# A prologue's row-max tiles over four PSUM banks instead of three, and a gelu's cube one step later

## The chip, the cores and the metric

The kernel runs on one core of one Trainium2 chip. The metric is the device time of one execution in microseconds (us). The engines are TensorE (PE in the profile; PEld is its weight load), VectorE (DVE), ScalarE (ACT), GpSimd (POOL) and SyncE (SP), which issues the DMAs. Each works through a queue of its own in order, and they wait for each other through semaphores.

## The reference, cut to what matters

```python
x = A_x                                          # (1, 2048, 640)
g = sigmoid((x * gate_w).sum(-1, keepdims=True))
q, k, v = heads(x @ wq), x @ wk, x @ wv          # 32 heads of 20; one k and one v for all heads
p = softmax(q @ k.T * 20 ** -0.5)
a = merge(p @ v) @ wo
h = layernorm(x)                                 # over the 640 channels
u = gelu(einsum("bsd,sf->bdf", h, w1) + b1)      # token mixing: F = 1728
b = transpose(einsum("bdf,fs->bds", u, w2) + b2)
return g * a + (1 - g) * b
```

All of it is float32. Products are made of a high part and a low part of each operand (three products of four).

## The kernel before, in words

**Three stages.** Up to about 96 us in the trace the kernel projects x to q, k, v and normalises it. Then comes a **prologue** (the loop over `fc in range(PRO)`, lines 574 to 601), about 72 us long, and after it the **main loop** (`main`, line 1017, and the blocks behind it), which holds the other 90% of the time. The change touches the prologue alone, and what its tiles leave to the main loop.

**The prologue's PE work.** It makes the first 8 (`PRO`) of 14 blocks of the first half of `u`. One pass of the loop is one block, `fc`: 4 quarters `hf` of 4 steps each, so 16 steps. A step is 6 matmuls (L586) on half the rows of the array each; `pu0` takes the upper rows, `pu1` the lower ones, and at the end of the pass the two are added. One weight chunk serves one quarter. `w1_upto` (line 118) prepares it three quarters ahead: a DMA brings `wr`; ScalarE rounds it to `wh` (L126; from chunk 32 on GpSimd does that, L128); GpSimd makes the rest `wl` = `wr` - `wh` (L129). So in each pass there are four chunks, called A, B, C and D here, prepared at steps 0, 4, 8 and 12.

**The row maxima.** Between steps, `lead` (line 569) starts two matmuls of q against k, 128x512 each (L479), and for each of them VectorE takes the maximum along the row (`tensor_reduce`, L482). There are 48 (`LEAD`) such pairs, so 96 tiles; one pair falls on each second or third step. The tiles come from `next_bank` (line 459), which in the prologue rotates over the pool `ps_m` of three banks. A tile can be written only after the reduction of the tile three earlier.

**PSUM.** The eight banks in the prologue: three for `ps_m`, one for `ps_g`, which stays unused until the main loop, and four for `pu0` and `pu1`, twice each (`psb`). In the main loop the four of `psb` become `ps_s` (three) and `ps_o` (one).

**The gelu.** At the end of each pass `gelu` (line 515) is called. ScalarE first takes `pu0` and the bias (called *bias* below, L519). The rest is put in the list `chain`, of which one entry is taken at the end of each following step (`pop_chain`), so it runs within the next pass. Its entries, with the short names used below:

- *add* (L525, VectorE, adds `pu1`) and right behind it *square* (L522, ScalarE)
- *cube* (L529, VectorE; `scalar_tensor_tensor` with two inputs in SBUF)
- *tanh* (L532, ScalarE)
- *product* (L545 and L546, GpSimd)
- *high* (L535, ScalarE, rounds to `u_hi`)
- *low* (L538, GpSimd)

A `None` is a step in which nothing of the gelu is issued. The last block's gelu (`fc == PRO - 1`) issues its add at once and has another chain, on GpSimd.

**The order of each queue** is thus the order in which the Python code issues (`manual_schedule` on all engines). ScalarE's queue in a pass is: wh of A, square, wh of B, tanh, wh of C, high, wh of D, then *bias* of this pass. GpSimd's is: wl of A, wl of B, product, wl of C, wl of D, low.

**The join.** The first tile from `ps_s` in the main loop (L479, tile `s`) takes a bank of `psb`, and so waits for the add of the last block's gelu, which waits for that block's *bias*, which stands on ScalarE behind *high* of the block before.

Of the kernel before, what the change touches and what calls it, by code (L numbers as in the profile page):

```python
# [9 lines left out]
F32 = mybir.dt.float32  # L10
# [4 lines left out]
PSUM = bass.MemoryType.PSUM  # L15
DRAM = bass.MemoryType.DRAM

P = 128
# [6 lines left out]
NB = 512  # L25
# [14 lines left out]
def mix_kernel(ctx: ExitStack, tc: tile.TileContext, A_x, A_wq, A_wk, A_wv, A_wo,  # L40
# [5 lines left out]
    def f32(ap):  # L46
        return ap.bitcast(F32)
# [30 lines left out]
    right = ExitStack()  # L78
# [39 lines left out]
    def w1_upto(n):  # L118
        while fetched[0] < min(n, len(chunks)):
            c = fetched[0]  # L120
            w1_load(c + 1)
            wr = w1raw[c]
            wh = w1p.tile([P, HS, P], F32R, name="wh")
            wl = w1p.tile([P, HS, P], F32R, name="wl")
            if c < 4 * PRO:
                nc.scalar.activation(wh, wr, AF.Copy)  # L126
            else:
                nc.gpsimd.tensor_copy(wh, wr)  # L128
            nc.gpsimd.tensor_sub(wl, wr, f32(wh))  # L129
            w1t[c] = wh, wl  # L130
            fetched[0] += 1
            w1_load(c + 4)
# [22 lines left out]
    def new_q(n):  # L155
        if n < NU:
            qtiles[n] = load_q(n, "qst")
# [289 lines left out]
    u_lo = [view(t, UC * HD2, UC) for t in (u0, slot[0])]  # L447
    pp_pool = ctx.enter_context(tc.tile_pool(name="pp", bufs=11))
    ev = ctx.enter_context(tc.tile_pool(name="ev", bufs=1))
    ps_m = ctx.enter_context(tc.tile_pool(name="ps_m", bufs=3, space=PSUM))  # L450
    ps_g = ctx.enter_context(tc.tile_pool(name="ps_g", bufs=1, space=PSUM))
    mpool = ctx.enter_context(tc.tile_pool(name="mpool", bufs=2))
    mmpool = ctx.enter_context(tc.tile_pool(name="mmpool", bufs=2))

# [3 lines left out]

    def next_bank():
        if not ring:  # L460
            return ps_m.tile([P, NB], F32, name="ms")
        ring[0] ^= 1
        return ps_m.tile([P, NB], F32, name="ms") if ring[0] else ps_s.tile([P, NB], F32, name="s")
    given = [0, 0]
# [2 lines left out]
    def ms_next(b):  # L467
        k = given[b]
        if k >= 32 * NU:
            return None  # L470
        given[b] += 1
        n, r = divmod(k, 32)
        (kq, pr), qt = divmod(r // 4, 2), r % 4

        def step():
            if n not in mtiles:
                mtiles[n] = mpool.tile([P, 16, 4], F32, name="mp")
            ms = next_bank()
            nc.tensor.matmul(ms, qmax[n][64 * b:64 * b + 60, pr, qt * P:(qt + 1) * P],  # L479
                             kst[64 * b:64 * b + 60, kq * NB:(kq + 1) * NB], start=True, stop=True)  # L480
            c = (2 * b + pr) * 4 + qt
            nc.vector.tensor_reduce(mtiles[n][:, c, kq:kq + 1], ms, axis=AX.X, op=ALU.max)  # L482
            issued[b] += 1
            if min(issued) == 32 * n + 1:
                new_qmax(n + 1)

        return step

    def ms_done():
        n = len(row_max)  # L490
        if n < NU and min(issued) >= 32 * (n + 1):
            mm = mmpool.tile([P, 16], F32, name="mm")
            nc.vector.tensor_reduce(mm, mtiles.pop(n), axis=AX.X, op=ALU.max)
            mn = mmpool.tile([P, 2, 16], F32R, name="mn")
            nc.gpsimd.tensor_scalar(mm, mm, -1.0, None, op0=ALU.mult)
            nc.gpsimd.tensor_copy(mn[:, 0, :], mm)
            nc.gpsimd.tensor_sub(mn[:, 1, :], mm, f32(mn[:, 0, :]))
            row_max[n] = mn

    def store_max(n):  # L500
        mn = row_max[n]
        mt = mpool.tile([P, 32], F32, name="mt")
        nc.vector.transpose(mt, f32(mn).rearrange("p j c -> p (j c)"))
        nc.sync.dma_start(out=m_scr[n], in_=mt)

    def fetch_max(n):
        src = m_scr[n].rearrange("(i j b r) e -> j b r i e", j=2, b=2, r=8)
        for b in range(2):
            for j in range(2):
                rows = f32(qtiles[n][64 * b + 60 + j:64 * b + 61 + j])  # L510
                nc.sync.dma_start(out=rows.rearrange("o p (t i e) -> o (p t) i e", i=4, e=32), in_=src[j, b][None])

    chain = []

    def gelu(d, fc, accs):
        both = fin.tile([P, D], F32, name="yo")
        xg, t1 = both[:, :HD2], both[:, HD2:]
        hi, lo = u_hi[d][:, fc, :], u_lo[d][:, fc, :]
        nc.scalar.activation(xg, accs[0][:, :HD2], AF.Identity, bias=bias[:, NS + fc:NS + fc + 1])  # L519

        def square():
            nc.scalar.activation(t1, xg, AF.Square)  # L522

        def add():
            nc.vector.tensor_add(xg, xg, accs[1][:, :HD2])  # L525
            square()

        def cube():
            nc.vector.scalar_tensor_tensor(t1, t1, 1.0 / 0.044715, xg, op0=ALU.add, op1=ALU.mult)  # L529

        def tanh():
            nc.scalar.activation(t1, t1, AF.Tanh, scale=GC * 0.044715)  # L532

        def high():
            nc.scalar.activation(hi, t1, AF.Copy)  # L535

        def low():
            nc.gpsimd.tensor_sub(lo, t1, f32(hi))  # L538

        def cube_p():  # L540
            nc.gpsimd.tensor_scalar(t1, t1, 1.0, 1.0 / 0.044715, op0=ALU.mult, op1=ALU.add)
            nc.gpsimd.tensor_mul(t1, t1, xg)

        def prod_p():
            nc.gpsimd.tensor_scalar(t1, t1, 1.0, 1.0, op0=ALU.mult, op1=ALU.add)  # L545
            nc.gpsimd.tensor_mul(t1, t1, xg)  # L546

        def high_p():
            nc.gpsimd.tensor_copy(hi, t1)
            nc.gpsimd.tensor_sub(lo, t1, f32(hi))  # L550

        if len(accs) == 2 and fc == PRO - 1:
            add()
            chain.extend((cube_p, None, tanh, prod_p, high_p))
        elif len(accs) == 2:
            chain.extend((None, None, add, None, cube, tanh, None, prod_p, None, None, None, high, None, low))
        else:
            chain.extend((square, cube_p, None, tanh, prod_p, high_p))

    def pop_chain():  # L560
        f = chain.pop(0) if chain else None
        if f:
            f()

    with tc.tile_pool(name="psb", bufs=2, space=PSUM, side="right") as psb:
        at, skip, last = 0, 3, NS * PRO - 6
        one_by_one[0] = True

        def lead():
            for b in range(2):  # L570
                ms_next(b)()
            ms_done()

        for fc in range(PRO):
            pu = [psb.tile([P, NB], F32, name=f"pu{r}") for r in range(2)]
            for hf in range(4):
                w1_upto(4 * fc + hf + 4)
                for f in [q_parts_due.pop(0) for _ in range(min(len(q_parts_due), 1 + fc // 5))] if fc else []:
                    f()
                wh, wl = w1t.pop(4 * fc + hf)  # L580
                for c in range(HS):
                    st = hf * HS + c
                    for k, (w, h) in enumerate(((wh, h_hi[0]), (wh, h_lo[0]), (wl, h_hi[0]))):
                        for r in range(2):
                            rows = slice(64 * r, 64 * r + 64)
                            nc.tensor.matmul(pu[r][:, :HD2], w[rows, c, :], h[rows, st, :],  # L586
                                             start=(st == 0 and k == 0), stop=(st == NS - 1 and k == 2))
                    done = [max(0, min(x, last) - skip) * LEAD // (last - skip) for x in (at, at + 1)]
                    if done[1] > done[0]:
                        lead()  # L590
                    at += 1
                    pop_chain()
                if fc == 1 and hf == 0:
                    new_q(0)
                if fc == PRO - 2 and hf == 2:
                    assert not q_parts_due
                    one_by_one[0] = False
                    fetch_max(0)
            gelu(0, fc, pu)
            if fc == PRO - 3:  # L600
                store_max(0)

    ps_s = ctx.enter_context(tc.tile_pool(name="ps_s", bufs=3, space=PSUM))
    ps_o = ctx.enter_context(tc.tile_pool(name="ps_o", bufs=1, space=PSUM))

# [558 lines left out]
```

## Time and profile before

| what | us |
|---|---|
| median of 3 runs | 1671.76 |
| lowest and highest | 1671.31, 1671.92 |
| the profiled execution | 1671.47 |
| its span in the trace | 1669.7 |
| prologue, first matmul of L586 to the start of the last | 96.5 to 168.1 |
| first matmul of tile `s` in the main loop | 169.53 |

All times in the text are counted from the start of the span. The granted TensorE clock is 1.00 throughout. In a row of the timeline the first number is the start and the second the length of one instruction or of a run of equal ones; what stands in square brackets is the idle time of the engine ahead of it and who ended it. Successive instructions of VectorE, ScalarE and GpSimd overlap a little: the next one starts before the row of the last one ends.

### The profile page before, as it was taken

What the parts mean: (1) busy time and instruction counts of PE and PEld (TensorE: products, weight loads), DVE (VectorE), ACT (ScalarE), POOL (GpSimd) and SP (SyncE); (2) the same over time, 40 slices, a digit from 0 to 9 for tenths busy, and PEclk for the clock granted to TensorE, in tenths of its full rate; (3) what the DMA queues carried; (4) which work ended last, traced back from release to release, by engine and by line L of the source; (5) the groups of instructions that cost most, each with busy time, mean ns of one, the idle gap of its engine ahead of it and who ended that gap; (6) DMA issues with size and microseconds to landing.
All of it is one profiled execution on the core that took longest, in us unless ns stands there. A gap on an engine that the chain in (4) does not pass through costs nothing.

```text
span 1669.7 us, 38827 instructions
## 1 busy us (share of the span) xinstructions
PE 1661.0 (99%) x14865; PEld 1105.5 (66%) x14865; DVE 1435.7 (86%) x2732; ACT 1188.0 (71%) x2346; POOL 606.3 (36%) x759
## 2 busy tenths in 40 slices
PE   9999999999999999999999999999999999999998
PEld 7899666666666666666666666666666566666665
DVE  6689899999989999988888988988888998988933
ACT  4434777777777777777777777777777777777775
POOL 6578555455455554422232332122122220111210
PEclk9999999999999999999999999999999999999999
DMA  7665222222132232222222222212222121333611
GB/s 211 205 176 137 79 71 69 78 58 78 53 84 73 71 82 74 58 60 62 66 75 74 55 62 66 61 52 71 63 66 60 55 65 41 96 111 113 189 51 39
DMA packets 178305, 138.20 MB, mean 83 GB/s; under 512 B 33306, under 2 KB 144055, under 8 KB 178119
## 3 DMA queue, kind: packets, MB, share of 16 engines
q1 hardware_dynamic: 177830, 135.39, 28.9%
q8 instruction: 117, 1.92, 0.5%
q14 instruction: 70, 0.57, 0.1%
q10 hardware_dynamic: 288, 0.33, 0.1%
HBM read 102.36 MB, written 31.65 MB: 80 GB/s over the span
## 4 chain that ended last, share of the span: by engine, by line
PE 95%; issue 2%; DVE 1%; SPq 1%; ACT 0%; DMA 0%; POOL 0%; POOLq 0%; DVEq 0%; ACTq 0%
PE o L684 28%; PE ms L479 18%; PE s L657 13%; PE g L750 10%; PE g L929 7%; PE ms L657 5%; PE pp L298 4%; PE s L479 3%; PE pu L586 3%; PE g L875 2%; DVE mp L482 1%; PE ms L831 0%; ACT p L660 0%; PE pt L290 0%; SPq L195 0%
## 5 line engine op out<-in xcount | busy, mean ns | idle before, releaser
L482 DVE TENSOR_REDUCE mp<-ms 128x1 f32<-128x512 f32 x1514 | 967.2, 685 | 130.2 <-PE ms L479 102.7
L660 ACT ACTIVATE p<-s 128x512 f32<-128x512 f32 x1512 | 820.6, 606 | 299.4 <-PE s L657 280.2
L479 PE MATMUL ms<-kst,qmx 60*128 60x512 f32 x1514 | 646.5, 433 | 1.7 <-DVE mp L482 1.7
L657 PE MATMUL s<-qst,kst 62*128 62x512 f32 x1512 | 601.6, 403 | 0.0
L684 PE MATMUL o<-p,v_sb 128*32 128x512 f32 x4096 | 511.3, 601 | 0.0
L479 PEld LDWEIGHTS ms<-kst,qmx 60*128 60x128 f32 x1514 | 279.0, 184 | 244.9 <-ACT p L660 114.7
L482 DVE TENSOR_REDUCE mp<-s 128x1 f32<-128x512 f32 x534 | 355.6, 683 | 12.0 <-PE s L479 11.8
L660 ACT ACTIVATE p<-ms 128x512 f32<-128x512 f32 x536 | 305.1, 599 | 56.8 <-PE ms L657 50.2
L657 PEld LDWEIGHTS s<-qst,kst 62*128 62x128 f32 x1512 | 278.5, 186 | 55.2 <-DVE flag L670 31.0
L929 PE MATMUL g<-slot,wh 64*128 64x320 f32 x1280 | 297.5, 311 | 0.0
L129 POOL TENSOR_TENSOR wl<-wr,wh 128x512 fp32r<-128x512 f32 x176 | 228.6, 1300 | 43.8 <-PE g L750 17.3
L479 PE MATMUL s<-kst,qmx 60*128 60x512 f32 x534 | 230.8, 441 | 0.4 <-DVE yo L525 0.4
L684 PEld LDWEIGHTS o<-p,v_sb 128*32 128x32 f32 x4096 | 97.5, 108 | 185.3 <-issue 177.2
L657 PE MATMUL ms<-qst,kst 62*128 62x512 f32 x536 | 216.8, 405 | 0.0
L929 PEld LDWEIGHTS g<-slot,wh 64*128 64x128 f32 x1280 | 211.6, 184 | 2.0 <-issue 1.7
L750 PE MATMUL g<-slot,wh 64*128 64x320 f32 x864 | 202.1, 313 | 0.1
L750 PE MATMUL g<-u,wh 64*128 64x320 f32 x864 | 201.7, 312 | 0.0
L929 PE MATMUL g<-slot,wl 64*128 64x320 f32 x640 | 199.6, 312 | 0.0
L706 POOL TENSOR_TENSOR ot<-ot,rl 128x512 f32<-128x512 f32 x30 | 31.6, 1052 | 346.6 <-DVE rl L705 346.6
L128 POOL CAST wh<-wr 128x512 fp32r<-128x512 f32 x144 | 88.3, 613 | 188.0 <-PE g L750 81.5
L750 PEld LDWEIGHTS g<-slot,wh 64*128 64x128 f32 x864 | 143.5, 184 | 4.9 <-ACT yo L758 4.0
L750 PEld LDWEIGHTS g<-u,wh 64*128 64x128 f32 x864 | 143.5, 184 | 1.1 <-issue 1.1
(202 smaller groups left out, 2092.8 us busy)
## 6 DMA issues: line engine op xcount, KB each, us to landing
wr<-in_B_w_dram SPq DMA_DIRECT2D x152, 256.0 KB
qmx<-q_scr SPq DMA_DIRECT2D x192, 80.0 KB
qst<-q_scr SPq DMA_DIRECT2D x192, 80.0 KB
slot<-o_scr SPq DMA_DIRECT2D x20, 320.0 KB
y_scr<-yo SPq DMA_DIRECT2D x16, 320.0 KB
o_scr<-oh SPq DMA_DIRECT2D x124, 40.0 KB
o_scr<-ol SPq DMA_DIRECT2D x124, 40.0 KB
q_scr<-qh SPq DMA_DIRECT2D x19, 256.0 KB
```

The source lines that it names most:

```text
L128: nc.gpsimd.tensor_copy(wh, wr)
L129: nc.gpsimd.tensor_sub(wl, wr, f32(wh))
L298: nc.tensor.matmul(pp, w, t, start=first and n == 0, stop=not more and n == len(steps) - 1)
L479: nc.tensor.matmul(ms, qmax[n][64 * b:64 * b + 60, pr, qt * P:(qt + 1) * P], kst[64 * b:64 * b + 60, kq * NB:(kq + 1) * NB], start=True, s ...
L482: nc.vector.tensor_reduce(mtiles[n][:, c, kq:kq + 1], ms, axis=AX.X, op=ALU.max)
L586: nc.tensor.matmul(pu[r][:, :HD2], w[rows, c, :], h[rows, st, :], start=(st == 0 and k == 0), stop=(st == NS - 1 and k == 2))
L657: nc.tensor.matmul(s, kst[64 * b:64 * b + 62, kb * P:(kb + 1) * P], q[64 * b:64 * b + 62, pr, :], start=True, stop=True)
L660: nc.scalar.activation(p, s, AF.Exp, scale=SCALE)
L684: nc.tensor.matmul(o[32 * hh:32 * hh + 32, :], v_sb[:, kb, :], ptiles.pop((u, hh)), start=(kb == 0), stop=(kb == NS - 1), skip_group_check ...
L750: other_tile(half, nc.tensor.matmul(hold["p"][:, :HD2], w[r, fc % HS, :], u[d][r, fc, :], start=(hold["n"] == 1), stop=(hold["n"] == 6 * F ...
L875: other_tile(half, nc.tensor.matmul(hold["p"][:, :HD2], o[r, c, :], w[r, c, d * HD2:(d + 1) * HD2], start=(hold["n"] == 1), stop=(hold["n" ...
L929: other_tile(half, nc.tensor.matmul(hold["p"][:, :HD2], w[r, st % HS, :], h[d][r, st, :], start=(hold["n"] == 1), stop=(hold["n"] == 6 * NS)))
```

## The change

```diff
-    ps_m = ctx.enter_context(tc.tile_pool(name="ps_m", bufs=3, space=PSUM))
-    ps_g = ctx.enter_context(tc.tile_pool(name="ps_g", bufs=1, space=PSUM))
...
     def next_bank():
         if not ring:
-            return ps_m.tile([P, NB], F32, name="ms")
+            return psl.tile([P, NB], F32, name="ml")
...
         elif len(accs) == 2:
-            chain.extend((None, None, add, None, cube, tanh, None, prod_p, None, None, None, high, None, low))
+            chain.extend((None, None, add, None, None, cube, tanh, None, prod_p, None, None, high, None, low))
...
-    with tc.tile_pool(name="psb", bufs=2, space=PSUM, side="right") as psb:
+    with tc.tile_pool(name="psl", bufs=4, space=PSUM) as psl, \
+            tc.tile_pool(name="psb", bufs=2, space=PSUM, side="right") as psb:
...
+    ps_m = ctx.enter_context(tc.tile_pool(name="ps_m", bufs=3, space=PSUM))
+    ps_g = ctx.enter_context(tc.tile_pool(name="ps_g", bufs=1, space=PSUM))
     ps_s = ctx.enter_context(tc.tile_pool(name="ps_s", bufs=3, space=PSUM))
```

The prologue's tiles (now called `ml`) come from a pool of four banks, `psl`, which takes the place of `ps_m` and `ps_g`; these two are opened behind the prologue, on the same banks. In the gelu's chain, cube, tanh and product each stand one step later than before; add, high and low stay at theirs. The lists of instructions on PE, ScalarE and SyncE keep their order. On VectorE the cubes of the second and of the fourth block stand behind four reductions after their add instead of two, that of the seventh behind two instead of none; the other four keep their place. On GpSimd the product of each of the seven blocks stands behind wl of C instead of ahead of it. The main loop's code is unchanged.

## The prediction

> **What bounds the kernel now.** First the windows: they say where TensorE is not full, and so where a change can count.
>
> ```profile
> core 0: us, PE busy (x) PEld busy (x) DVE busy (x) ACT busy (x) POOL busy (x), PEclk, DMA share, GB/s
> 96.00:168.00 72.00, 70.28 (x866) 67.66 (x866) 67.50 (x120) 29.36 (x58) 57.39 (x58) 1.00 0.56 154
> 168.00:180.00 12.00, 11.59 (x105) 8.52 (x105) 8.89 (x17) 9.12 (x19) 9.82 (x12) 1.00 0.60 158
> 180.00:200.00 20.00, 20.00 (x188) 13.14 (x185) 18.02 (x37) 14.96 (x31) 7.23 (x11) 1.00 0.12 35
> 400.00:1500.00 1100.00, 1099.81 (x9982) 705.78 (x9980) 990.84 (x1879) 819.75 (x1611) 346.99 (x441) 1.00 0.24 67
> ```
>
> The main loop (last two rows) has PE busy throughout and GpSimd idle for two thirds, so it passes on one for one what the prologue ends earlier or later, and takes up lateness of GpSimd. In the prologue (first row) PE lacks 1.7 us, but VectorE is busy 67.5 of 72 and GpSimd 57.4. Next the list of waits of 96 to 170 us:
>
> ```profile
> ACT u L535 <- POOL yo L546: 10.8, 7, 1.6
> PEld ms L479 <- DVE mp L482: 3.1, 5, 1.4
> PE ms L479 <- DVE mp L482: 1.7, 4, 1.1
> ```
>
> PE and its weight load wait in the prologue for reductions alone: a third bank isn't free. The first row matters later: *high* waits about 1.5 us for the product in each of 7 passes.
>
> How much could PE gain? Three neighbouring pairs from the chain of waits:
>
> ```profile
> 102.05 0.37 PE ms L479 x2
> ...
> 104.73 0.37 PE ms L479 x2
> ...
> 107.40 0.37 PE ms L479 x2
> ```
>
> ```profile
> 106.21 1.19 PE pu L586 x16
> ...
> L586 PE MATMUL pu<-slot,wh x512: 301/305/418, 96.5 to 167.9; 64*128 64x320 f32 x171
> ```
>
> Two pairs with their 5 steps take 2.68 undisturbed, and 16 matmuls 1.19, so a step of six 0.45. The 48 pairs with 120 steps are 24 x 2.68 = 64.3, the 8 other steps 3.6: 67.9 us. From 96.5 PE would end at 164.4 instead of 168.1: **3.7 us** is all that banks can give.
>
> **The change: the fourth bank.** VectorE's share of a pass:
>
> ```profile
> 102.31 2.48 DVE L482 TENSOR_REDUCE mp<-ms 128x1 f32<-128x512 f32 x4 [0.19 <-PE ms L479]
> 115.60 0.48 DVE L525 TENSOR_TENSOR yo<-yo,pu 128x320 f32<-128x320 f32 x1
> 115.99 1.28 DVE L482 TENSOR_REDUCE mp<-ms 128x1 f32<-128x512 f32 x2
> 117.19 0.48 DVE L529 SCALAR_TENSOR_TENSOR yo<-yo 128x320 f32<-128x320 f32 x1
> ```
>
> Four reductions take 2.48, 0.60 from start to start; add and cube push the next one back by 0.4 each. Per 2.68 of PE VectorE thus needs 2.40, and the 0.8 of the gelu is caught up in three such periods of a pass. With three banks the second tile of a pair waits for the first reduction of the pair just before; with four for that of the second last, one reduction (0.60) more of slack. That covers add or cube alone, and the two together in part. Taken alone the edit is worth nearly the 3.7 us.
>
> **The change: cube, tanh and product one step later.** No instruction is added. A cube that follows two more reductions is late by 1.2 us in the second and fourth block. In the seventh it no longer waits for *square* (0.54 in the row of 162.63 below). All this would be small, but the product now stands behind wl of C on GpSimd, and that closes a ring. The rows of the first gelu, GpSimd and then ScalarE:
>
> ```profile
> 108.96 1.65 POOL L129 TENSOR_TENSOR wl<-wr,wh 128x512 fp32r<-128x512 f32 x1 [1.72 <-ACT wh L126]
> 110.58 0.46 POOL L545 TENSOR_SCALAR yo<-yo 128x320 f32<-128x320 f32 x1
> 111.12 0.88 POOL L546 TENSOR_TENSOR yo<-yo 128x320 f32<-128x320 f32 x1
> 111.96 2.54 POOL L129 TENSOR_TENSOR wl<-wr,wh 128x512 fp32r<-128x512 f32 x2
> 114.46 0.88 POOL L538 TENSOR_TENSOR u<-yo,u 128x320 fp32r<-128x320 f32 x1
> 115.30 1.30 POOL L129 TENSOR_TENSOR wl<-wr,wh 128x512 fp32r<-128x512 f32 x1
> 117.18 1.65 POOL L129 TENSOR_TENSOR wl<-wr,wh 128x512 fp32r<-128x512 f32 x1 [0.58 <-ACT wh L126]
> ```
>
> ```profile
> 112.03 0.47 ACT L535 ACTIVATE u<-yo 128x320 fp32r<-128x320 f32 x1 [1.55 <-POOL yo L546]
> 112.41 0.62 ACT L126 ACTIVATE wh<-wr 128x512 fp32r<-128x512 f32 x1
> ...
> 116.48 0.61 ACT L126 ACTIVATE wh<-wr 128x512 fp32r<-128x512 f32 x1
> ```
>
> From start to start a wl takes 1.25, *low* 0.84; the product takes 1.42 from its start to its end (110.58 to 112.00). *High* begins 0.03 later, wh of D 0.38 after that and lasts 0.62, and wl follows 0.08 behind its wh (116.48 + 0.61 to 117.18). So from the product's end to wl of D it is 1.11. Before, wl of C ran in that time. Now wl of C has gone ahead, and GpSimd stands idle. Its pass becomes 1.11 + 1.25 (D) + 0.84 + 3 x 1.25 (A, B, C) + 1.42 = **8.37**, against PE's (67.9 / 8) 8.5: no slack is left, and one more thing is on the ring, the tanh ahead of wh of C, and so the cube. The cube meets GpSimd:
>
> ```profile
> 66.61 1.15 DVE L242 TENSOR_TENSOR r<-r 128x4 f32<-128x4 f32 x1
> 67.80 0.16 DVE L243 TENSOR_TENSOR r<-r,ve 128x4 f32<-128x4 f32 x1
> 162.63 0.78 DVE L529 SCALAR_TENSOR_TENSOR yo<-yo 128x320 f32<-128x320 f32 x1 [0.54 <-ACT yo L522]
> ```
>
> ```profile
> 66.46 1.29 POOL L129 TENSOR_TENSOR wl<-wr,wh 128x512 fp32r<-128x512 f32 x1 [2.31 <-ACT wh L126]
> 161.76 1.29 POOL L129 TENSOR_TENSOR wl<-wr,wh 128x512 fp32r<-128x512 f32 x1
> ```
>
> An operation worth 0.16 that began 0.15 behind a wl ended with it, and the cube that began inside a wl ended 0.36 behind it (163.41 and 163.05). Where cube and wl begin together (117.19 and 117.18), the wl pays, 1.65 instead of 1.29. Before, that is the usual case. Now GpSimd runs without gaps and the cube falls into the middle of a wl. I take it that it waits to that wl's end. [...]
>
> Now the passes, by the product's end. First: wl of C at 110.58, product at 111.83, end **113.25**.
>
> - *Second (cube behind four reductions).* wl of D 114.36, low 115.61, wl of A 116.45, of B 117.70 to 118.99. Add at 115.5, about as before; cube 0.4 + 4 x 0.60 later, at 118.3, inside that wl, so it ends 119.35. Tanh 119.38, wh of C 119.76 to 120.38, wl of C 120.46, product 121.71 to **123.13**: 9.88.
> - *Third (two reductions).* wl of D 124.24, low 125.49, A 126.33 to 127.62. *Bias* stands behind high and wh of D, so it starts at 123.13 + 0.41 + 0.38 = 123.9, and the add comes at 125.3, as before. Cube 1.6 later at 126.9, inside A, ends 127.98; tanh 128.01; wh of C 128.39 to 129.01; wl of C 129.09, 0.26 later than GpSimd could; product ends **131.76**: 8.63.
> - The fourth is as the second, 9.88; the sixth as the third, 8.63. The fifth has three small GpSimd operations more (L495 to L497, 0.86 together, which swallow the 0.26): 9.23. In the seventh GpSimd also rounds two chunks (L128, 0.68 each, 1.36): 8.37 + 1.36 and some 0.15 of cube: 9.9.
>
> Sum: 113.25 + 2 x 9.88 + 2 x 8.63 + 9.23 + 9.9 = **169.40**, against 165.41 before:
>
> ```profile
> 164.54 0.87 POOL L546 TENSOR_TENSOR yo<-yo 128x320 f32<-128x320 f32 x1
> 168.37 0.53 ACT L519 ACTIVATE yo<-pu,bias 128x320 f32<-128x320 f32 x1 [2.46 <-PE pu L586]
> 168.99 0.49 DVE L525 TENSOR_TENSOR yo<-yo,pu 128x320 f32<-128x320 f32 x1 [2.00 <-ACT yo L519]
> 169.53 0.49 PE L479 MATMUL s<-kst,qmx 60*128 60x512 f32 x1 [0.41 <-DVE yo L525]
> ```
>
> Before, the last *bias* waited for PE. Now it stands behind *high*: 169.40 + 0.03 + 0.38 = 169.81, and tile `s` comes 1.16 behind it as here, at **170.97** instead of 169.53. Behind the waiting `s` all of PE's queue stands still. So PE's gain, wherever it is had, is spent waiting at the join, and **1.4 us** are lost. The profiled execution takes 1671.47 (1.8 of it around the span), so 1672.9; it lies 0.3 under the median of 1671.76 and inside the runs' spread.
>
> Other edits at nothing: `ps_m` and `ps_g` opened later start on banks whose reductions end ahead of 168, under the same wait of PE; the product's lateness touches chunks 33 and 34, whose wl would end near 168 and 171.4 and which the main loop needs behind `s`. If that cover fails, it costs what the chunk is late, at most the few tenths that GpSimd's order leaves.
>
> **The rivals.**
>
> - *The gain stays* (1671.47 - 3.7 = **1667.8**): the ring does not bind and PE ends freely. For it: all PE waits in the list are for banks. [...] Against: wl of C was what filled GpSimd's 1.11, and it is taken out. 0.10.
> - *The cube doesn't wait for wl.* The long passes are then: cube ends 118.78, tanh 118.81, wl of C 119.89, 0.57 sooner, so 9.3; short ones 8.37, with the small operations 8.95, the last 9.73. The product ends at 167.3, `s` comes at 168.8, 0.7 sooner than before: **1670.7**. Against: the two rows. 0.14.
> - *The other side: VectorE loses each encounter.* GpSimd's next instruction is queued already, so the cube could lose a full wl in every pass, from the second on, once GpSimd has no gap. Six passes of 9.88 and 0.58 for the small operations: 113.25 + 59.86 = 173.1, `s` at 174.7, 5.1 later: **1676.6**. Two of the three short passes would do to bring it over 1675.1 (9.88 - 8.63 each). For it: no gap is left before C. Against: at 162.63 it lost 0.30 only, and in short passes tanh hides part. 0.10.
> - That the tiles don't rotate over four would leave the ring's loss and PE's waits together; it would give the forecast's time or some tenths more, and is in its range.
>
> **How the numbers follow.** Forecast 0.66 (1672 to 1674 by itself: add and cube may stand 0.6, one reduction, to either side in each long pass), rivals 0.10, 0.14, 0.10. The range leaves out the first rival and the last, 0.2 together: 1670.4 to 1674.8. A measurement of this kernel tells about 0.2% (3.3 us) from no change: faster is under 1668.4, most of the first rival, 0.08; slower over 1675.1, most of the last, 0.09; the rest, 0.83, is the same.
>
> **What would show it.** In the profile after: product (the line of L546) ending near 113.3, 123.1, 131.8 and 169.4; GpSimd idle about 1.1 ahead of wl of D, ended by wh; VectorE's cubes of 0.8 to 1.1 us instead of 0.48; the last *bias* released by *high* and not by PE; PE idle for about 3 us ahead of the first `s`, and that near 171.0. Wrong would be: `s` ahead of 169, with no such idle time (the ring had slack), or products 8.4 apart (no encounter), or PE waiting for reductions as before (the banks did nothing).

## The result and the profile after

| | before | after |
|---|---|---|
| median of 18 runs each (us) | 1671.58 | 1674.47 |
| lowest to highest | 1671.03 to 1671.92 | 1673.72 to 1675.47 |
| profiled execution; its span | 1671.47; 1669.7 | 1675.47; 1673.7 |

The ratio is 1.0017, 95% interval 1.001 to 1.0024: slower by 2.9 us. The forecast was 1672.9, with a range of 1670.4 to 1674.8. The profiled execution of after is the slowest of its 18, and its prologue begins 0.61 later than before's (97.06 and 96.45, ahead of everything that the change touches), so places in the prologue are compared from the first matmul of L586 (L585 in the changed kernel, whose line numbers stand 1 or 2 off).

The waits of 96 to 172 us of the changed kernel (who waited, for whom; us in total, times, longest):

```profile
ACT u L533 <- POOL yo L544: 23.4, 7, 4.6
...
DVE yo L523 <- ACT yo L517: 3.7, 1, 3.7
...
PE s L477 <- DVE yo L523: 3.2, 1, 3.2
...
PEld ml L477 <- DVE mp L480: 1.2, 3, 0.4
```

PE's waits for the banks of the row maxima are down to 1.2 from 4.8 (its own and its weight load's). *High* now waits 23.4 for the product instead of 10.8, and at the join `s` waits 3.2 for the last add (0.4 before), and that add for the last *bias*. GpSimd in the first three passes that hold a gelu, in the sixth, and at the end:

```profile
109.57 2.89 POOL L129 TENSOR_TENSOR wl<-wr,wh 128x512 fp32r<-128x512 f32 x2 [1.76 <-ACT wh L126]
112.43 0.45 POOL L543 TENSOR_SCALAR yo<-yo 128x320 f32<-128x320 f32 x1
112.97 0.87 POOL L544 TENSOR_TENSOR yo<-yo 128x320 f32<-128x320 f32 x1
114.94 1.29 POOL L129 TENSOR_TENSOR wl<-wr,wh 128x512 fp32r<-128x512 f32 x1 [1.10 <-ACT wh L126]
...
117.03 2.55 POOL L129 TENSOR_TENSOR wl<-wr,wh 128x512 fp32r<-128x512 f32 x2
121.04 1.29 POOL L129 TENSOR_TENSOR wl<-wr,wh 128x512 fp32r<-128x512 f32 x1 [1.46 <-ACT wh L126]
...
122.83 0.87 POOL L544 TENSOR_TENSOR yo<-yo 128x320 f32<-128x320 f32 x1
...
126.90 4.04 POOL L129 TENSOR_TENSOR wl<-wr,wh 128x512 fp32r<-128x512 f32 x3
...
131.44 0.88 POOL L544 TENSOR_TENSOR yo<-yo 128x320 f32<-128x320 f32 x1
...
154.77 4.04 POOL L129 TENSOR_TENSOR wl<-wr,wh 128x512 fp32r<-128x512 f32 x3
...
169.28 0.86 POOL L544 TENSOR_TENSOR yo<-yo 128x320 f32<-128x320 f32 x1
```

The idle time of 1.10 ahead of wl of D is there, ended by wh, and in the second pass 1.46 more ahead of wl of C, which waits for the late cube by way of tanh and wh. In the third and in the sixth pass the wl of A, B and C follow each other without a gap, but take 4.04 (the two of 117.03 take 2.55, and a third from start to start 1.25). VectorE's cubes of the first, second, third and sixth block, and then ScalarE at the end:

```profile
109.58 0.48 DVE L527 SCALAR_TENSOR_TENSOR yo<-yo 128x320 f32<-128x320 f32 x1
...
118.79 1.14 DVE L527 SCALAR_TENSOR_TENSOR yo<-yo 128x320 f32<-128x320 f32 x1
...
127.42 1.11 DVE L527 SCALAR_TENSOR_TENSOR yo<-yo 128x320 f32<-128x320 f32 x1
...
154.65 0.52 DVE L527 SCALAR_TENSOR_TENSOR yo<-yo 128x320 f32<-128x320 f32 x1
```

```profile
170.17 0.47 ACT L533 ACTIVATE u<-yo 128x320 fp32r<-128x320 f32 x1 [4.64 <-POOL yo L544]
170.54 0.51 ACT L517 ACTIVATE yo<-pu,bias 128x320 f32<-128x320 f32 x1
```

The cubes of 1.1 are those that came into a wl; they end 0.35 behind it. The last *bias* has no wait of its own: it stands behind *high*, and *high* behind the product. PE at the join, and then three windows around it (columns: window, length, busy time and instructions of PE, PEld, DVE, ACT, POOL, granted clock, DMA share, GB/s):

```profile
167.47 0.49 PE L477 MATMUL ms<-kst,qmx 60*128 60x512 f32 x1 [0.27 <-DVE mp L480]
...
171.68 0.79 PE L477 MATMUL s<-kst,qmx 60*128 60x512 f32 x1 [3.21 <-DVE yo L523]
```

```profile
165.00:171.50 6.50, 3.20 (x36) 2.68 (x32) 2.77 (x6) 1.36 (x3) 6.18 (x8) 1.00 0.46 124
171.50:174.90 3.40, 3.22 (x18) 3.22 (x19) 2.11 (x4) 1.74 (x4) 3.24 (x5) 0.50 0.47 131
174.90:180.00 5.10, 5.10 (x46) 3.19 (x44) 3.85 (x8) 4.78 (x10) 3.41 (x5) 1.00 0.64 180
```

The middle row was not forecast: behind the idle time the granted clock is 0.50 for 3.41 us, and `s` itself takes 0.79 instead of 0.49.

### The profile page after: what moved, and what is told of

Its sections match the earlier page's. It is cut to its first block, busy times and chain, and to the rows that moved or that the text cites. A ratio compares the mean times of both kernels' runs of the same rounds, so it can differ in the third digit from the quotient of the medians.

```text
span 1673.7 us, 38827 instructions
## 1 busy us (share of the span) xinstructions
PE 1662.6 (99%) x14865; PEld 1107.0 (66%) x14865; DVE 1437.6 (86%) x2732; ACT 1186.9 (71%) x2346; POOL 604.6 (36%) x759
## 4 chain that ended last, share of the span: by engine, by line
PE 92%; DVE 4%; issue 2%; DMA 1%; SPq 0%; ACT 0%; POOL 0%; POOLq 0%; DVEq 0%
PE o L685 28%; PE ms L477 17%; PE s L658 13%; PE g L751 10%; PE g L930 7%; PE ms L658 5%; PE pp L298 4%; DVE mp L480 3%; PE s L477 3%; PE g L876 2%; PE ms L832 0%; PE pp L362 0%; PE pu L585 0%; PE pt L290 0%; DMA xa<-in_A_x_dram 0%
## 5 line engine op out<-in xcount | busy, mean ns | idle before, releaser
L480 DVE TENSOR_REDUCE mp<-ms 128x1 f32<-128x512 f32 x1418 | 908.2, 686 | 127.7 <-PE ms L477 100.5
L477 PE MATMUL ms<-kst,qmx 60*128 60x512 f32 x1418 | 615.7, 435 | 0.3 <-DVE mp L480 0.3
L477 PEld LDWEIGHTS ms<-kst,qmx 60*128 60x128 f32 x1418 | 261.8, 185 | 241.5 <-ACT p L661 114.5
```

## The experiments

**Theory A**: the product behind wl of C closes a ring through *high* and wh of D, which sets the pace and keeps the last *bias*, and so `s`, back. **Rival B**: the late cube that meets a wl is the cause, wherever the product stands. **Rival C**: nothing but the half clock behind the idle time. (These letters have nothing to do with the chunks, which are always called wl of A, wh of D and so on.)

The table counts from the first matmul of the prologue in each profile: the start of the prologue's last matmul, the end of the seventh product, the start of `s`, and of the 101st exponential of the main loop (a fixed place some 70 us behind the join); then PE's idle time ahead of `s`, and how long the clock stood at 0.50 behind it. Times are medians; each ratio is to runs of the kernel before on the same chip. The medians of those runs differ by up to 0.9 (1671.58 for after, 1672.32 for e1 to e4, 1672.48 for e5 to e7, 1671.64 for e8 to e10), so times of different chips are compared by their ratios, and small steps by the places within the profile.

| kernel | PE end | product | `s` | 101st exp | idle | half clock | time | ratio (95%) |
|---|---|---|---|---|---|---|---|---|
| before | 71.63 | 68.95 | 73.08 | 144.74 | 0.41 | 0 | 1671.58 | 1 |
| after | 69.83 | 73.07 | 74.62 | 147.38 | 3.21 | 3.41 | 1674.47 | 1.0017 (1.001 to 1.0024) |
| e1_banks | 69.48 | 67.39 | 70.93 | 142.61 | 0.41 | 0 | 1669.68 | 0.9983 (0.9974 to 0.9992) |
| e2_chain | 73.18 | 72.92 | 74.63 | 146.34 | 0.41 | 0 | 1673.23 | 1.0006 (0.9997 to 1.0015) |
| e3_prod_stays | 67.73 | 67.41 | 69.19 | 140.89 | 0.35 | 0 | 1667.65 | 0.9972 (0.9962 to 0.9983) |
| e4_prod_alone | 70.15 | 71.18 | 72.73 | 145.31 | 1.55 | 3.41 | 1671.64 | 0.9997 (0.9988 to 1.0006) |
| e5_fill | 69.88 | 73.16 | 74.72 | 146.41 | 0.30 | 0 | 1673.00 | 1.0004 (0.9995 to 1.0013) |
| e6_one_input | 67.91 | 70.70 | 72.25 | 144.56 | 3.30 | 3.41 | 1671.53 | 0.9997 (0.9988 to 1.0006) |
| e7_high_late | 67.76 | 68.65 | 70.20 | 142.57 | 1.33 | 3.41 | 1669.82 | 0.9984 (0.9975 to 0.9993) |
| e8_after_again | 69.78 | 73.06 | 74.61 | 147.37 | 3.23 | 3.41 | 1674.36 | 1.0016 (1.0007 to 1.0024) |
| e9_fill8 | 69.82 | 73.10 | 74.64 | 146.33 | 1.22 | 0 | 1673.02 | 1.0008 (0.9999 to 1.0017) |
| e10_fill4 | 69.79 | 73.04 | 74.58 | 146.93 | 2.12 | 3.41 | 1673.79 | 1.0012 (1.0003 to 1.0021) |

**The two halves of the change, each alone.** e1_banks is after with the old chain:

```diff
-            chain.extend((None, None, add, None, None, cube, tanh, None, prod_p, None, None, high, None, low))
+            chain.extend((None, None, add, None, cube, tanh, None, prod_p, None, None, None, high, None, low))
```

> Four banks, the chain of before. Theory A (the ring through the product behind wl of C makes the loss): the product is ahead of wl of C again, GpSimd has its slack, so the gain of the banks shows: tile s 1.8 to 3.7 us earlier than before, the time 1668.0 to 1669.8, no idle time of over 1 us ahead of s, the granted clock 1.00 throughout. Rival B (a cube that meets a wl is what costs, wherever the product stands): the cubes begin together with wl of B as before, so B expects the same gain here. Rival C (nothing but the half clock behind the idle time): the same gain.

The banks alone gain 2.1 us at `s` and 0.9983 in time, near the lower end. It tells nothing between A and B. What the fourth bank leaves is seen on VectorE in the last pass, where cube waits for *square* and then for a wl:

```profile
159.32 0.47 DVE L523 TENSOR_TENSOR yo<-yo,pu 128x320 f32<-128x320 f32 x1
160.33 1.30 DVE L527 SCALAR_TENSOR_TENSOR yo<-yo 128x320 f32<-128x320 f32 x1 [0.54 <-ACT yo L520]
```

e2_chain is before with the new chain (the diff the other way round, on three banks).

> Three banks, the new chain. A: the ring sets the pace as in the changed kernel, the product of the last block ends near 169.5, s comes 1.5 to 1.9 us later than before; but PE has spent the time within the prologue on reductions (about 5 us of waits instead of 3.5), so it idles for under 1 us at the join and keeps its clock: 1.5 to 2 us slower than before, 1673.1 to 1673.6. C: no idle time at the join, no half clock, so no loss: 1671.6.

`s` comes 1.55 later than before, the 101st exponential 1.60, and there is no half clock: as A has it, and C falls as the only cause (the new chain costs 1.55 without any). The time by itself, 1.0006, is too near to 1 to tell. PE ends its prologue 1.55 later too, so it spent the time there on banks, as expected. The chain sets the same pace with three banks as with four: the product ends at 72.92 and 73.07. That settles which half decides.

**Which of the three moved entries.** e3_prod_stays, and below it e4_prod_alone, both on four banks:

```diff
-            chain.extend((None, None, add, None, None, cube, tanh, None, prod_p, None, None, high, None, low))
+            chain.extend((None, None, add, None, None, cube, tanh, prod_p, None, None, None, high, None, low))
```

> Four banks, cube and tanh one step later, the product at its old step, ahead of wl of C. A: GpSimd's idle time of 1.1 ahead of wl of D is filled by wl of C again, the ring opens, PE runs freely and s comes 3.5 us earlier than before: 1668.0. B: the cubes of the second and fourth block still come 1.2 later and fall inside a wl, so 0.6 to 1.2 us are lost in each long pass and the time is 1671 to 1674.

```diff
-            chain.extend((None, None, add, None, None, cube, tanh, None, prod_p, None, None, high, None, low))
+            chain.extend((None, None, add, None, cube, tanh, None, None, prod_p, None, None, high, None, low))
```

> Four banks, cube and tanh at their old steps, the product alone one step later, behind wl of C. A: the ring is closed (8.4 to 8.7 a pass) but without the two late cubes; s comes within 0.5 us of before, though PE ends its passes earlier and idles 1.5 to 2 us at the join; with a half clock behind it up to 0.7 more: 1671.2 to 1672.5, and some 3 us slower than the banks alone. B: the cubes are where they were, so the gain of the banks stays: 1668.0 to 1669.8.

With the product ahead of wl of C, PE runs freely and `s` comes 3.89 earlier than before, ratio 0.9972: the fastest version here, and faster than both kernels. That the cube is late does not cost by itself: the cubes of the second and fourth block come as late as in after, and take 0.48. They touch only the last 0.08 of a wl, though, so what a full encounter costs is not tested here. The timeline of VectorE in the second block:

```profile
115.60 0.47 DVE L523 TENSOR_TENSOR yo<-yo,pu 128x320 f32<-128x320 f32 x1
116.00 2.47 DVE L480 TENSOR_REDUCE mp<-ml 128x1 f32<-128x512 f32 x4
118.39 0.48 DVE L527 SCALAR_TENSOR_TENSOR yo<-yo 128x320 f32<-128x320 f32 x1
```

In e4_prod_alone, with the product alone moved, 3.89 shrinks to 0.35 at `s`. B's 1668.0 to 1669.8 is missed, A's 1671.2 to 1672.5 hit (1671.64), though the distance to e1_banks is 2.0 and not some 3: the product's place is what costs the gain. This run doesn't part the ring from the encounter. With GpSimd's queue shifted, the cubes at their old steps meet a wl all the same, in the second, fourth and sixth block (1.07, 1.12 and 1.04), which A had not expected either; the rows of the second:

```profile
116.61 1.07 DVE L527 SCALAR_TENSOR_TENSOR yo<-yo 128x320 f32<-128x320 f32 x1
```

```profile
116.05 4.04 POOL L129 TENSOR_TENSOR wl<-wr,wh 128x512 fp32r<-128x512 f32 x3
```

**Out of the ring by another door.** e7_high_late leaves product and cubes late, and moves *high* behind wh of D on ScalarE:

```diff
-            chain.extend((None, None, add, None, None, cube, tanh, None, prod_p, None, None, high, None, low))
+            chain.extend((None, None, add, None, None, cube, tanh, None, prod_p, None, None, None, None, high, None, low))
```

> The changed kernel with high two steps later, behind wh of D on ScalarE (and low two steps later). The product stays behind wl of C, the cubes stay late. A: wh of D no longer waits for high, so wl of D follows the product at once, the 1.1 of idle time in each pass is gone and the ring has slack; PE runs freely to 164.7, the last product ends about 165.5 and s comes 2.4 us earlier than before: 1669.2, without a half clock or with a short one. B (late cubes): 1673 to 1674.5.

`s` comes 2.88 earlier than before (2.4 expected), the time is 1669.82. The cubes of the second and fourth block are as late as in after and take 0.48. So it is the link from the product by way of *high* to wh of D that matters, and not the lateness of cube or product as such. PE idles 1.33 at the join, and even that halves the clock:

```profile
166.18 0.50 PE L477 MATMUL s<-kst,qmx 60*128 60x512 f32 x1 [1.33 <-DVE yo L523]
```

```profile
166.00:168.00 2.00, 1.82 (x13) 1.82 (x15) 1.41 (x3) 0.94 (x2) 1.92 (x4) 0.68 0.09 18
168.00:170.00 2.00, 2.00 (x12) 1.96 (x12) 0.81 (x3) 1.82 (x5) 1.83 (x3) 0.50 0.98 265
170.00:172.00 2.00, 2.00 (x24) 2.00 (x23) 1.88 (x4) 2.00 (x5) 1.21 (x2) 0.97 0.75 211
```

**The cube's encounter with wl.** e6_one_input takes the cube's second operand from PSUM:

```diff
-        nc.vector.scalar_tensor_tensor(t1, t1, 1.0 / 0.044715, xg, op0=ALU.add, op1=ALU.mult)
+        nc.vector.scalar_tensor_tensor(t1, t1, 1.0 / 0.044715, accs[1][:, :HD2], op0=ALU.add, op1=ALU.mult)
```

> The changed kernel, but the cube multiplies by pu1 in PSUM instead of by the block in SBUF (so the gelu's values are others), and has one input in SBUF. A with the encounter of the two engines as a part of the ring: cubes take 0.48 everywhere and no wl 1.65, the product of the last block ends 2.0 to 2.2 earlier, s comes 2 us earlier, about 0.5 ahead of before; PE still idles over 3 us at the join and pays the half clock: 1671.8 to 1672.5. If the encounter isn't what lengthens the passes, the time stays at 1674.5.

```profile
117.86 0.47 DVE L527 SCALAR_TENSOR_TENSOR yo<-yo,pu 128x320 f32<-128x320 f32 x1
...
126.16 0.48 DVE L527 SCALAR_TENSOR_TENSOR yo<-yo,pu 128x320 f32<-128x320 f32 x1
```

```profile
116.10 2.54 POOL L129 TENSOR_TENSOR wl<-wr,wh 128x512 fp32r<-128x512 f32 x2
119.44 1.29 POOL L129 TENSOR_TENSOR wl<-wr,wh 128x512 fp32r<-128x512 f32 x1 [0.81 <-ACT wh L126]
...
123.22 1.30 POOL L129 TENSOR_TENSOR wl<-wr,wh 128x512 fp32r<-128x512 f32 x1 [1.10 <-ACT wh L126]
```

The cube of 117.86 runs in 0.47 in the middle of the wl of 117.35, and the product ends 2.37 earlier than in after (2.0 to 2.2 expected; the time, 1671.53, is just under the 1671.8 to 1672.5 expected). The encounter is real and is worth 2.4 us; the idle time of 1.10 is left, so the ring stands without it, and `s` is only 0.83 ahead of before. This is the run that parts the two: of the 5.43 by which `s` comes later in after than in e3_prod_stays, 3.06 are the ring without an encounter, and 2.37 are encounters. Rival B is thus a part of the loss, but only where the ring is closed: in e3_prod_stays and e7_high_late the same late cubes of the second and fourth block lost nothing. The half clock takes most of the 0.83 back (the 101st exponential is 0.18 ahead of before's).

**The half clock.** e5_fill, e9_fill8 and e10_fill4 put 12, 8 and 4 matmuls that nobody needs between prologue and main loop; e8_after_again is after, unaltered:

```diff
     ps_o = ctx.enter_context(tc.tile_pool(name="ps_o", bufs=1, space=PSUM))
+    fill = ps_m.tile([P, NB], F32, name="ms")
+    for i in range(12):
+        nc.tensor.matmul(fill, kst[:, :P], kst[:, :NB], start=True, stop=True)
```

> The changed kernel with 12 matmuls of 128x512 between prologue and main loop whose result nobody reads; they run while PE waits for s. A: s comes when it came (171.7 in the profile, some 1.5 behind before's when counted from the first matmul of the prologue), but PE hasn't idled for 3.2 us, so the granted clock stays 1.00 behind it, and the time is about 1.1 us shorter than that of the changed kernel: 1673.3. If the half clock has nothing to do with the idle time, the time stays at 1674.5 or grows.

> The changed kernel once more, unaltered, beside the next two on the same chip. 2.4 to 3.2 us slower than before; PE idle 3.2 us ahead of s, the clock at 0.50 for 3.4 us behind it.

> The changed kernel with 8 matmuls at the join instead of 12, so that PE still idles about 1.2 us ahead of s (3.2 less 8 x 0.25). If it takes an idle time of between 1.12 (before, clock kept) and 1.33 us (e7_high_late, clock halved) to halve the clock, this stands at the border: with the clock kept the time is that of 12 matmuls, some 1.3 us under the changed kernel; with it halved for 3.41 us, that of the changed kernel.

> The changed kernel with 4 matmuls at the join: PE still idles about 2.2 us. If the half clock is a thing of a fixed length once PE has idled too long, it lasts 3.41 us here as well, and the time is that of the changed kernel, within 0.3 us; if its length goes with the idle time, a third of the loss is won back, 0.4 us.

The row of `s` in e5_fill, in e9_fill8 and in e10_fill4:

```profile
171.20 0.50 PE L477 MATMUL s<-kst,qmx 60*128 60x512 f32 x1 [0.30 <-DVE yo L523]
```

```profile
170.96 0.50 PE L477 MATMUL s<-kst,qmx 60*128 60x512 f32 x1 [1.22 <-DVE yo L523]
```

```profile
170.79 0.50 PE L477 MATMUL s<-kst,qmx 60*128 60x512 f32 x1 [2.12 <-DVE yo L523]
```

In all four `s` comes at 74.6 to 74.7. With 12 and with 8 matmuls the clock stays at 1.00 and the 101st exponential comes 1.0 earlier than in after (146.41 and 146.33 for 147.37); beside e8_after_again on the same chip, e9_fill8 saves 1.34 us. So extra work on a waiting engine shortened the kernel. With 4 matmuls the clock is halved for 3.41 again, which speaks for a fixed length, but 0.57 is won back all the same (0.44 at the 101st exponential), which neither expectation had. There the half clock begins 1.34 behind `s` (172.13 and 170.79; the granted clock of 170 to 172, 172 to 174 and 174 to 176 is 1.00, 0.53 and 0.61), in after 0.18 ahead of it (171.50 and 171.68), so it falls on other work. That this is why it costs less is not shown.

## Why the prediction was right or wrong

*What the banks can give at most, 3.7.* Nearly right: 3.89 in e3_prod_stays, 0.2 over it.

*"Taken alone the edit is worth nearly the 3.7 us."* Mis-sized: 2.15 at `s`. The text had it that 0.60 of slack covers add or cube alone "and the two together in part"; what stayed uncovered was larger than "nearly" allowed. In e1_banks the list of waits still has rows of 1.6 and 0.9 for banks, in e3_prod_stays, where the cube comes a step later, none; the cube of the seventh block even took 1.30 instead of 0.78. The sum didn't rest on it, since the ring spends it anyway.

*The ring.* Right. Ends of the products from the prologue's first matmul, forecast (less 96.45) and measured: 16.80 and 16.78; 26.68 and 26.64; 35.31 and 35.26; 72.95 and 73.07 for the seventh. GpSimd's idle time was forecast as 1.11 and is 1.10. e3_prod_stays and e7_high_late, which open it at two places, and e6_one_input, which leaves it closed without an encounter, show that the link product, *high*, wh of D carries it.

*The encounters.* Right for the second and the fourth pass: the cube came into a wl, took 1.14 and 1.18, and both passes are 9.86 long, 9.88 forecast. In the third and the sixth the length is right, 8.62 for 8.63, by luck. The forecast had the late cube hold up wl of C by 0.26, by way of tanh and wh, in both. In the trace GpSimd has no idle time ahead of wl of C in either; instead one wl took 1.54 in place of 1.29, in the third the one behind the cube of 1.11, in the sixth the one that began 0.13 after a cube of 0.52. The second rival's condition, made in e6_one_input, gave about what it was priced at: `s` 0.83 sooner than before, 0.7 forecast. (The rivals' sums count the small operations of the fifth pass as 0.58, the forecast as 0.86; with 0.86 the second rival would have had `s` 0.4 sooner.) What the forecast took from the rows of 66.61 and 162.63, that a cube waits to the end of the wl it comes into, held: the cube of 118.79 ended 0.35 behind its wl. Where the two begin together (109.57 and 109.58), it is again the wl that pays, 2.89 for two instead of the 2.55 of 117.03.

*The join.* Right: `s` 1.54 later than before, 1.44 forecast, released by the last *bias* behind *high*.

*The step that failed:* that the main loop "passes on one for one what the prologue ends earlier or later". It passed on 1.54 as 2.64 at the 101st exponential. PE's idle time of 3.2, which the prediction had named, has a price behind it: the half clock, 1.0 to 1.1. Forecast 1.44 and this 1.05 make 2.5 of the 2.9; the rest is inside what e8_after_again's runs differ by (1673.74 to 1674.93). That the time stayed inside the range, 0.33 below its upper end, was luck in part: the range was drawn for the place of add and cube, and this price was not in it. The rivals: the first happens when the product stays (`s` 3.89 earlier, forecast 3.7), so it was a matter of one entry of a list; the third did not (passes of 8.62 stand between those of 9.86).

*Other edits at nothing.* Held as far as seen: the first tile of `ps_m` waits 0.27 for the last reduction, under the wait for `s`, and behind that wait the list of PE's waits from 171 to 260 has no row for a late chunk.

## What to carry to other kernels

Before moving a step by one place, follow it through every queue that it stands in, and ask what it was hiding: here wl of C filled the time that *high* and wh of D take behind the product, and once it went ahead, GpSimd, with 20% of free time on the average before (57.39 of 72 busy), set the pace. A buffer more helps only as far as no such ring is closed elsewhere; move the two edits of a change apart before judging either. And price an idle stretch of TensorE at a join with what its clock does behind it: here 0.50 for 3.41 us, which cost 0.6 to 1.1 by the 101st exponential.

## What the runs showed of the hardware

An idle time of TensorE ahead of `s` of 1.33 (e7_high_late), 1.55 (e4_prod_alone), 2.12 (e10_fill4) or 3.21 to 3.30 us (after, e8_after_again, e6_one_input) was followed by a granted clock of 0.50 for 3.41 us; with 1.22 (e9_fill8), and with 1.12 (before) and 1.04 (e2_chain) within the prologue, there was none. From `s` to the 101st exponential the runs without a half clock take 71.7, those with one 0.6 to 1.1 more. The half clock began 1.8 us (e4_prod_alone: idle from 167.26, half clock from about 169.08, worked out from the mean of 0.77 of 168 to 170) to 4.8 us (e6_one_input: idle from 165.08, half clock from about 169.84, from the mean of 0.96) behind the start of the idle time. In the 3.41 just ahead of the half clock TensorE was busy for 0.38 (after, 168.09 to 171.50) to 2.08 (e7_high_late, 3.41 less the idle 1.33). No run has an idle time between 1.22 and 1.33 there, so where the border lies, and whether the length of the idle time alone sets it, is open.

The cube, a VectorE operation that here has two inputs in SBUF, ended 0.35 behind the GpSimd `tensor_tensor` (wl) that it came into: in after 118.79 + 1.14 = 119.93, and the wl of 118.28 ends at 119.58; in e1_banks 160.33 + 1.30 = 161.63, and the wl of 159.99 ends at 161.28. With one input in SBUF and one in PSUM it ran in 0.47 within a wl (e6_one_input, 117.86).
